# Attention and two MLPs on one core: the first decays' row transfers move from SyncE's queue to ScalarE's, and the loads of weights are released from waiting for them

## The chip, the cores and the metric

The kernel runs on one core of one Trainium2 chip. The metric is the device time of one execution in microseconds (us); lower is better.

## What is computed

For 4 batches of 8 heads, 576 positions and head size 64: scores = q k^T / 8 plus a decay, `cum[s] - cum[t]`, where `cum` is the running sum of `log(clip(f, 1e-4, 1))`; a causal mask; softmax; times v. The result is laid out as 2304 tokens of 512 values and goes through two MLPs:

```
scores = where(causal, -1e9, scale * q @ k.T + cum[:, None] - cum[None, :])
x = softmax(scores) @ v                                  # 2304 x 512
x = relu(x @ w_in).pow2 @ w_out                          # MLP 1, 512 -> 2048 -> 512
out = relu(x @ w2_in).pow2 @ w2_out                      # MLP 2
```

The weights arrive in 64 bit and are decoded to 32 bit by VectorE in the kernel.

## The kernel before, in words

**Matmuls.** Each number of an MLP is split into a high and a low part (fp32r), and three products of parts replace one. MLP 1 runs over groups of 256 tokens (`mlp_a`); for each of 16 tiles of 128 hidden units it does 12 matmuls (L844), a relu, square and split on ScalarE, GpSimd and VectorE, and 12 matmuls (L919). MLP 2 (L1213, L1239) follows in three units of 768 tokens.

**Stages of the attention.** The positions of a sequence are cut at 0, 64, 192, ... The first 64 positions of all heads are done by two calls of `first_part(y)` (y = 0, 1, two batches each), the next 128 by 16 calls of `pair`, the rest by 32 calls of `unit`. The two first parts together make the 256 tokens of MLP 1's group 0. The decay enters the scores as two more rows of q and k (rows 64 and 65 of a 66-row contraction): `load_qk` loads 64 rows (512 KB for each y), and `load_aug(r)` copies row 64 + r from `a0`, which lies on 32 partitions, to one partition (8 KB each, four in all). `a0` comes from `f` by clip, log (ScalarE), running sum (`scan0`, VectorE) and two multiplications by 8 and -8 (`times8`, L1325). After the scores (L481) a first part takes eight steps of softmax (L487 to L497), a transpose (L509) and its copy (L512), the product with v (L521), and the split into `xk` (L536 on ScalarE, L538 on VectorE). Then L844 can start on group 0.

**Weights.** `weights(i)`, i = 0 to 15, loads 1 MB (128 x 2048 words) with SyncE (L784), decodes it in three VectorE operations (L802, L804, L806), rounds on ScalarE (L819) and subtracts on VectorE (L823). Three staging tiles serve the loads. Loads 1 and 2 have `first_loads[:2]` as dependencies, the two transfers of y = 0's decay rows. Load 0 depends on `o_t`, the loading of ScalarE's first table. The `qk` loads of `pair` depend on all four decay transfers, and so does `store2`, which writes the pairs' decays to DRAM.

**The order of work.** Every operation is entered by `op(engine, duration, fn, priority, deps, buffers)`. `Plan.run` simulates the engines with these durations, and emits the instructions of each engine in the order in which they started in the simulation. The lowest priority number goes first: `U` is -1.0e9, the first parts stand at -1.0e8, load i of the weights at -459.5 + 133.3 i, the pairs at 201.5 i. An engine holds a slot free for an operation of priority below -1.0e7 only if that is ready within 0.1 us of simulated time. On the chip each engine runs its instructions in that fixed order. While the plan finds TensorE idle it puts in small matmuls that nobody reads (L1360).

Of the kernel before, what the change touches and what calls it, by code (L numbers as in the profile page):

```python
# [69 lines left out]
class Plan:  # L70
# [17 lines left out]
    def op(self, eng, dur, fn, prio, deps=(), uses=(), data=None, other=None, dmas=1, rows=128):  # L88


        o = Op()
        o.how, o.uses, o.data, o.dmas, o.rows, o.turn = {eng: (dur, fn, 0)}, tuple(uses), data, dmas, rows, dur == self.TURN[0]
        if other:
            o.how[other[0]] = (other[1], other[2], 1)
        o.prio = (prio, len(self.ops))
        o.outs, o.ready, o.nwait = [], 0.0, 0
        for d in deps:
            if d is not None:
                d.outs.append(o)
                o.nwait += 1  # L100
        for b in o.uses:
            b.left += 1
        self.ops.append(o)
        return o

    def run(self):
# [15 lines left out]
        while todo:  # L122
            again = True
            while again:
                again = False
                for e in engs:
# [60 lines left out]
                    end = t + dur + self.LAT[e]  # L187
                    if o.data is not None:

                        free[e] = t  # L190
                        _, a, z = self.TURN if o.turn else self.COPY
                        for _ in range(o.dmas):
                            at = max(free[e], lanes[issued % 8])
                            free[e] = at + dur / o.dmas
                            dge = max(dge, at) + a
                            dma = max(dma, dge + z) + o.data / o.dmas
                            end = lanes[issued % 8] = dma + self.LAT["DMA"] + (self.TURNED if o.turn else 0.0)
                            issued += 1
# [60 lines left out]
def attention_then_two_squared_relu_mlps(  # L259
# [15 lines left out]
    nc = tc.nc  # L275
# [177 lines left out]
    def first_part(y, prio):  # L453
# [10 lines left out]
            nc.sync.dma_start(out=room[y][0:64], in_=qk0[y])  # L464

        def load_aug(r):
            nc.sync.dma_start(out=qk_[64 + r:65 + r].rearrange("p n z s -> p n (z s)"),
                              in_=a0[2 * y * H:2 * y * H + 2 * H, r].rearrange("p z s -> p (z s)"))

        def load_v():  # L470
            nc.sync.dma_start(out=vv, in_=v0[y])

        l1 = op("SP", P.COPY[0], load_qk, U + y, first_loads[:2] if TUNE["q1"] else [], data=1.46)
        l2 = [op("SP", P.COPY[0], lambda r=r: load_aug(r), U + 1 + y, [aug_first], data=0.1) for r in range(2)]
        first_loads.extend(l2)
        l3 = op("SP", P.COPY[0], load_v, U + 3 + y, l2, data=0.73)

        def sc():
            for b, i, h in heads:
# [1 line left out]
                nc.tensor.matmul(bk()[64 * h:64 * h + 64, c:c + Q0], lhsT=qk_[:66, n, 0], rhs=qk_[:66, n, 1],  # L481
                                 start=True, stop=True, skip_group_check=True)

        e = op("PE", 1.24, sc, prio, [l1] + l2, [bk], rows=66)
        full = [128, H, Q0]
        steps = [
            ("DVE", dve(512), lambda: nc.vector.scalar_tensor_tensor(  # L487
# [34 lines left out]
                                 rhs=pT[rows, 128 * i + 64 * h:128 * i + 64 * h + 64],  # L522
                                 start=True, stop=True, skip_group_check=True)

        e = op("PE", 1.24, av, prio, [e, l3], [o, t], rows=64)
        first_done.append(e)

        for b in range(2):
# [17 lines left out]
    def pair(b, i, prio):  # L546


        h0 = 2 * i
        x, vv, pp, pT, bk, o = Buf(QKA), Buf(VV), Buf(PP), Buf(PTA), Buf(BK), Buf(BO)  # L550
        n = QA - Q0
        p0 = pos(b, Q0)

        def v_():
            return vv().rearrange("p n z d -> p (n z d)")[:, 0:3 * D].rearrange("p (n d) -> p n d", n=3)

        def load_qk():
            nc.sync.dma_start(out=x()[0:64], in_=qk[b, h0:h0 + 2, :, :QA].rearrange("h (z d) s -> d (h z) s", z=2))

        def load_aug():  # L560
            nc.sync.dma_start(out=x()[64:66], in_=aug2_d[:, b * H + h0:b * H + h0 + 2].rearrange("r h z s -> r (h z) s"))

        def load_v():
            nc.sync.dma_start(out=v_(), in_=v1[b, i])

        ld = op("SP", P.COPY[0], load_qk, prio, first_loads, [x], data=0.6)
        o_aug = op("SP", P.COPY[0], load_aug, prio, aug_second + [ld], [x], data=0.1)
        ov = op("SP", P.COPY[0], load_v, prio + TUNE["vd"], [ld], [vv], data=0.55)

        def sc():  # L570
            y = x()
            for h, c, k0, k1 in ((0, 0, 0, QA), (1, QA, 128, QA), (1, QA + 64, 0, 128)):
                nc.tensor.matmul(bk()[:, c:c + k1 - k0], lhsT=y[:66, 2 * h, Q0:QA], rhs=y[:66, 2 * h + 1, k0:k1],
                                 start=True, stop=True, skip_group_check=True)

        o_s = op("PE", 0.84, sc, prio, [ld, o_aug], [x, bk], rows=66)
        os_ = []
        for t in range(2):
            c = slice(QA * t, QA * t + QA)
            e = op("DVE", dve(QA) + 0.01, lambda t=t, c=c: max_of(pp, t, bk()[:, c], mask1[:, c], c.start),  # L580
                   prio, [o_s, o_m1], [bk, pp])
            os_.append(op("ACT", act(QA) + 0.18, lambda t=t: exp_of(pp, t, 128, QA * t, QA), prio, [e], [pp]))
        o_r = op("DVE", 0.07, lambda: recip(0, pp, 0, 2, 1.0), prio, os_, [pp])
        o_r = op("DVE", 0.08, lambda: recip(1, pp, 0, 2), prio, [o_r], [pp])

        def norm(eng, t):
            y, r = pp()[0][:, QA * t:QA * t + QA], pp()[3][:, t:t + 1]
            if eng == "ACT":
                nc.scalar.activation(out=y, in_=y, func=AF.Copy, scale=r)
            else:  # L590
                (nc.vector if eng == "DVE" else nc.gpsimd).tensor_scalar(out=y, in0=y, scalar1=r, scalar2=None, op0=ALU.mult)

        p_ops = [either(TUNE["pha"], *((e, d, lambda t=t, e=e: norm(e, t)) for e, d in (("ACT", act(QA) + 0.09), ("DVE", dve2(QA) + 0.06))),
                        prio, [o_r], [pp], c=("POOL", pool_(QA), lambda t=t: norm("POOL", t))) for t in range(2)]

        def tr():
            for j in range(3):
                c = slice(128 * j, 128 * j + 128)
                nc.tensor.transpose(o()[:, c], pp()[0][:, c], ident)

        def copy(eng):
            (nc.scalar.copy if eng == "ACT" else nc.vector.tensor_copy)(out=pT()[:, 0:384], in_=o()[:, 0:384])

        o_tr = op("PE", 0.375, tr, prio, p_ops, [pp, o])
        a_tr.append(o_tr)
        o_tr = either(TUNE["ev"], ("ACT", act(384, True), lambda: copy("ACT")), ("DVE", dve(384), lambda: copy("DVE")),
                      prio + TUNE["pz"], [o_tr], [o, pT])

        def av():
            y = pT()  # L610
            for h in range(2):
                rows, dst = slice(64 * h, 64 * h + 64), o()[64 * h:64 * h + 64, 384:512]
                nc.tensor.matmul(dst, lhsT=v_()[:, h], rhs=y[:, 256 * h:256 * h + 128],
                                 start=True, stop=False, skip_group_check=True)
                nc.tensor.matmul(dst[:, 64:128], lhsT=v_()[rows, 2], rhs=y[rows, 192:256],
                                 start=False, stop=True, skip_group_check=True)

        o_av = op("PE", 0.8, av, prio + TUNE["pq"], [o_tr, ov], [pT, vv, o])
        a_av.append(o_av)

        def fold(eng):
            dst = X[:, i, p0:p0 + n]
            (nc.scalar.copy if eng == "ACT" else nc.vector.tensor_copy)(out=dst, in_=o()[:, 384:512])

        e = either(TUNE["fa"], ("ACT", act(n, True), lambda: fold("ACT")), ("DVE", dve(n), lambda: fold("DVE")),
                   prio + TUNE["fo"], [o_av], [o])
        for g in groups(p0, p0 + n):
            fold_ops.setdefault((g, i), []).append(e)
# [144 lines left out]
    def weights(i, prio, prio2, deps, free, stage, words):  # L773
# [47 lines left out]
        def lo(eng):  # L821
# [1 line left out]
            eng.tensor_tensor(out=x[:, 1::2], in0=word(), in1=f32(x[:, 0::2]), op=ALU.subtract)  # L823

        o = either(2 if i < TUNE["ws"] else TUNE["wq"], ("SP", P.COPY[0], lambda: load(nc.sync)), ("ACT", 0.15, lambda: load(nc.scalar)),
                   prio, deps + (first_loads[:2] if i else []), [st], data=2.92 if wide else 1.46)
        if wide:
            for y in range(3 if t is not st else 4):
                o = op("DVE", dve2(1024) if y in ((0,) if t is not st else (0, 2)) else dvs(1024),
# [433 lines left out]
    with tc.manual_schedule():  # L1263
# [56 lines left out]
            nc.vector.tensor_tensor_scan(out=f_cum[:, 0:z], data0=f_log[:, 0:z], data1=zero.to_broadcast([nh_, z]), initial=0.0,  # L1320
                                         op0=ALU.add, op1=ALU.add)

        def times8(x, n):
            for i, m in enumerate((8.0, -8.0)):
                nc.vector.tensor_scalar(out=x[:, i, i], in0=f_cum[:, 0:n], scalar1=m, scalar2=None, op0=ALU.mult)  # L1325

        def scan0():
            scan(Q0)
            times8(a0, Q0)

        def scan1():
            scan(S)
# [35 lines left out]
        o = op("ACT", act(Q0), lambda: f_ln(0, Q0), U, [o])  # L1368
        o_f = op("DVE", dve2(S - Q0), lambda: f_clip(Q0, S), -1.0e7, [o_f])
        o_f = op("ACT", act(S - Q0), lambda: f_ln(Q0, S), U, [o_f])  # L1370
        op("ACT", 1.5, lambda: nc.scalar.activation(out=stat[:, 0, 0, 6:7], in_=stat[:, 0, 0, 7:8], func=AF.Exp), U, [o_f])
        aug_first = o = op("DVE", 0.45, scan0, U, [o, o_c])
        first_done, first_loads = [], []
        for y in range(2):
            first_part(y, -1.0e8 + y)
        o = op("DVE", 0.67, scan1, -1.0e7, [o_f])
        o_8 = op("ACT", 2 * act(QA), times8_act, -1.0e7, [o, o_m1])
        aug_second = [op("SP", P.COPY[0], store2, -1.0e7, [o_8] + first_loads, data=0.3)]
        o_p = op("ACT", act(S), lambda: parts(0), TUNE["PP"], [o] + first_done)
        o_p = op("DVE", dvs(S), lambda: parts(1), TUNE["PP"], [o_p])  # L1380
        o_p = op("ACT", 2 * act(S), lambda: parts(2), TUNE["PP"], [o_p])
# [116 lines left out]
```

## Time and profile before

| | us |
|---|---|
| runs | 997.28, 1000.00, 1002.94 (median 1000.0) |
| profiled execution | 1000.74 |
| its span, first to last instruction | 999.0 |
| TensorE busy | 969.2 |
| VectorE busy | 674.8 |
| ScalarE busy | 458.2 |
| GpSimd busy | 328.5 |
| mean granted clock | 0.986 of full |

A busy time is the sum over instructions, overlaps counted once; matmuls are pipelined, so that a busy TensorE is not one at its peak. The clock is the share of full speed that TensorE was granted.

### The profile page before, as it was taken

The numbers are of one execution on the slowest core, as the hardware profiler recorded it, in microseconds if no ns is written. First come the engines' busy times: TensorE is split into PE (matmuls) and PEld (weight loads), VectorE is DVE, ScalarE is ACT, GpSimd is POOL, SyncE is SP. The second block draws the span as 40 slices with busy tenths as digits, with TensorE's granted clock in tenths as the row PEclk, the third lists the DMA queues.
The fourth block names the chain that finished last, engine by engine and source line by source line (L and its number), as shares of the span: only waits on it lengthen the run. The fifth ranks groups of instructions, "written<-read, shape, count | busy, mean of one in ns | idle before, by whom it ended". The sixth has DMA issues, their size and how long they took to land.

```text
span 999.0 us, 17472 instructions
## 1 busy us (share of the span) xinstructions
PE 969.2 (97%) x6697; PEld 865.5 (87%) x6699; DVE 674.8 (68%) x1355; ACT 458.2 (46%) x894; POOL 328.5 (33%) x270
## 2 busy tenths in 40 slices
PE   5999999999999999999999999999999999999997
PEld 3788898788888888887999999898988989889896
DVE  6989666767667766666278689978684435844343
ACT  2776566778677767776333354222231112311111
POOL 2211242544243424334232343124252223522220
PEclk6999999999999999999999999999999999999999
DMA  9766146666656656655547712753333222232223
GB/s 266 241 190 234 43 96 127 131 123 132 142 109 140 148 108 140 127 118 119 115 148 231 234 43 89 271 195 120 127 114 140 70 78 64 87 104 68 77 67 106
DMA packets 172948, 131.93 MB, mean 132 GB/s; under 512 B 134784, under 2 KB 151424, under 8 KB 170688
## 3 DMA queue, kind: packets, MB, share of 16 engines
q1 hardware_dynamic: 172864, 130.81, 48.5%
q8 instruction: 53, 0.87, 0.4%
q14 instruction: 31, 0.25, 0.1%
HBM read 85.07 MB, written 18.42 MB: 104 GB/s over the span
## 4 chain that ended last, share of the span: by engine, by line
PE 38%; issue 7%; DVE 3%; POOL 3%; ACT 1%; DMA 0%; POOLq 0%; SPq 0%; DVEq 0%; ACTq 0%
PE hp L1213 13%; PE bk L1239 10%; PE yp L919 5%; PE hp L844 5%; PE yp L1239 5%; POOL g L1226 2%; DVE w L1102 1%; PE bk L740 1%; POOL gt L869 0%; DVE sq L856 0%; DVE X L1082 0%; ACT w L1100 0%; DVE w L1147 0%; DMA out_dram<-st 0%; DMA qk<-aug_d 0%
## 5 line engine op out<-in xcount | busy, mean ns | idle before, releaser
L919 PE MATMUL yp<-gt,w 128*128 128x256 f32 x1728 | 229.0, 281 | 1.4 <-POOL gt L869 1.4
L844 PE MATMUL hp<-xk,w 128*128 128x256 f32 x1728 | 224.4, 280 | 0.2 <-DVE w L823 0.2
L919 PEld LDWEIGHTS yp<-gt,w 128*128 128x128 f32 x1728 | 215.9, 188 | 2.9 <-POOL gt L869 1.8
L844 PEld LDWEIGHTS hp<-xk,w 128*128 128x128 f32 x1728 | 212.2, 188 | 1.0 <-DVE w L823 0.4
L869 POOL TENSOR_TENSOR gt<-sq,gt 128x512 fp32r<-128x512 f32 x72 | 100.3, 1393 | 208.7 <-ACT gt L866 193.3
L1239 PE MATMUL bk<-w,g 128*128 128x512 f32 x576 | 148.2, 394 | 0.2 <-POOL g L1226 0.2
L1226 POOL TENSOR_TENSOR g<-r,g 128x768 fp32r<-128x768 f32 x34 | 63.5, 1868 | 211.3 <-ACT g L1225 209.4
L1213 PE MATMUL hp<-w 128*128 128x384 f32 x630 | 125.1, 338 | 3.4 <-DVE r L1190 3.4
L1225 ACT CAST g<-r 128x768 fp32r<-128x768 f32 x48 | 40.1, 836 | 187.1 <-DVE r L1224 187.0
L1213 PEld LDWEIGHTS hp<-w 128*128 128x128 f32 x630 | 113.3, 190 | 11.1 <-issue 2.3
L1239 PEld LDWEIGHTS bk<-w,g 128*128 128x128 f32 x576 | 106.7, 188 | 17.8 <-POOL g L1226 0.6
L412 ACT ACTIVATE pp<-pp,stat 128x448 f32<-128x448 f32 (+1 forms) x128 | 78.4, 613 | 36.0 <-DVE stat L404 26.4
L434 DVE SCALAR_TENSOR_TENSOR ph<-pp,stat,ph 128x320 f16<-128x320 f32 (+2 forms) x96 | 71.0, 741 | 27.3 <-ACT ph L427 26.1
L404 DVE CUSTOM_DVE_ANT_0 pp<-bk,mask 128x448 f32<-128x448 f32 (+1 forms) x128 | 59.9, 472 | 40.4 <-PE bk L700 38.7
L1190 DVE TENSOR_TENSOR r<-hp,st 128x384 f32<-128x384 f32 x64 | 35.5, 555 | 67.9 <-PE hp L1213 67.8
L1224 DVE SCALAR_TENSOR_TENSOR r<-r 128x768 f32<-128x768 f32 x48 | 78.4, 1632 | 1.5
L740 PE MATMUL bk<-pt,vv 64*128 64x64 f16 (+7 forms) x672 | 78.1, 254 | 0.0
L1213 PE MATMUL hp<-w,far 128*128 128x384 f32 x378 | 74.4, 335 | 0.0
L1239 PE MATMUL yp<-w,g 128*128 128x512 f32 x288 | 74.4, 393 | 0.0
L427 ACT ACTIVATE ph<-pp,stat 128x320 f16<-128x320 f32 (+2 forms) x96 | 63.8, 665 | 17.8 <-DVE stat L421 13.7
L1213 PEld LDWEIGHTS hp<-w,far 128*128 128x128 f32 x378 | 67.3, 188 | 4.9
L740 PEld LDWEIGHTS <-vv 128*128 128x128 bf16 (+3 forms) x672 | 37.1, 101 | 39.6 <-issue 25.6
(170 smaller groups left out, 1227.3 us busy)
## 6 DMA issues: line engine op xcount, KB each, us to landing
w<-wo_d SPq DMA_DIRECT2D x48, 512.0 KB
stage<-in_w_dram SPq DMA_DIRECT2D x26, 512.0 KB
raw<-in_qk_dram SPq DMA_DIRECT2D x32, 288.0 KB
wo_d<-part SPq DMA_DIRECT2D x16, 512.0 KB
st<-in_w_dram SPq DMA_DIRECT2D x7, 1024.0 KB
ph<-in_w_dram SPq DMA_DIRECT2D x7, 1024.0 KB
vv<-in_v_dram SPq DMA_DIRECT2D x32, 160.0 KB
qk_a<-in_qk_dram SPq DMA_DIRECT2D x16, 192.0 KB
```

The source lines that it names most:

```text
L404: nc.vector.tensor_tensor_reduce(out=x[:rows, c0:c0 + wd], in0=src, in1=msk, scale=-0.125, scalar=3.0e38 if first else nmax[:rows, 5:6], o ...
L412: nc.scalar.activation(out=x, in_=x, func=AF.Exp, scale=-1.0, bias=nmax[:rows, t:t + 1], accum_out=ssum[:rows, t:t + 1])
L427: nc.scalar.activation(out=a, in_=x, func=AF.Copy, scale=r)
L434: nc.vector.scalar_tensor_tensor(out=flat[:rows, z:z + wd], in0=x, scalar=r, in1=flat[:rows, 128 * blk:128 * blk + wd], op0=ALU.mult, op1= ...
L740: nc.tensor.matmul(dst.rearrange("p (n c) -> p n c", n=rh.shape[1]), lhsT=lt, rhs=rh, start=(i == 0), stop=(i == len(todo) - 1), skip_grou ...
L844: nc.tensor.matmul(ps, lhsT=lt, rhs=rh, start=(k_ == 0 and c == 0), stop=(k_ == KD - 1 and c == 2))
L869: eng.tensor_tensor(out=gt[1]()[:, :c], in0=sq()[:, :c], in1=f32(gt[0]()[:, :c]), op=ALU.subtract)
L919: nc.tensor.matmul(yp[d // 2]()[:, d % 2], lhsT=lt, rhs=rh, start=(i == 0 and c == 0 and d % 2 == 0), stop=(i == NF - 1 and c == 2), skip_ ...
L1213: nc.tensor.matmul(ps()[:, 0:TH], lhsT=lt, rhs=rh, start=(k_ == 0 and c == 0), stop=(k_ == 1 and c == 2))
L1224: o = op("DVE", dvs(TU), lambda r=r: nc.vector.scalar_tensor_tensor(out=r(), in0=r(), scalar=0.0, in1=r(), op0=ALU.max, op1=ALU.mult), e0, ...
L1226: l = either_vp(TU, lambda e, r=r, g=g: e.tensor_tensor(out=g()[:, 1], in0=r(), in1=f32(g()[:, 0]), op=ALU.subtract), e0, [h], [r, g])
L1239: nc.tensor.matmul(bank(ob[c]), lhsT=g()[:, a, c * 128:(c + 1) * 128], rhs=rw()[:, b], start=(p == 0 and x == 0 and z == 0), stop=(p == NP ...
```

## The change

The four decay transfers are issued by ScalarE. Row 64's needs VectorE's multiplication, row 65's needs a new one on ScalarE (`scan0_act`). No load of weights, no `qk` load of a pair and no `store2` depends on them any more; `v0[y]` follows the plan's landing of `qk0[y]`. Load 0 of the weights has priority U + 0.5 in place of -459.5. The load of ScalarE's Exp table goes to U + 1.5. Four durations in the plan are lowered: the scores and the product with v of a first part, and the transposes and the product with v of a pair. In the planner a transfer that isn't issued by SyncE occupies its engine for the duration given and does not pass through the simulated transfer queue.

```diff
-                    if o.data is not None:
+                        if e != "SP":
+                            end = t + dur + o.data + self.LAT["DMA"]
+                    if o.data is not None and e == "SP":
 ...
-            nc.sync.dma_start(out=qk_[64 + r:65 + r].rearrange("p n z s -> p n (z s)"),
+            nc.scalar.dma_start(out=qk_[64 + r:65 + r].rearrange("p n z s -> p n (z s)"),
 ...
-        l1 = op("SP", P.COPY[0], load_qk, U + y, first_loads[:2] if TUNE["q1"] else [], data=1.46)
-        l2 = [op("SP", P.COPY[0], lambda r=r: load_aug(r), U + 1 + y, [aug_first], data=0.1) for r in range(2)]
-        first_loads.extend(l2)
-        l3 = op("SP", P.COPY[0], load_v, U + 3 + y, l2, data=0.73)
+        l1 = op("SP", P.COPY[0], load_qk, U + y, data=1.46)
+        l2 = [op("ACT", P.COPY[0], lambda r=r: load_aug(r), U + y, [aug_first[r]], data=0.1) for r in range(2)]
+        l3 = op("SP", P.COPY[0], load_v, U + 3 + y, [l1], data=0.73)
 ...
-        e = op("PE", 1.24, sc, prio, [l1] + l2, [bk], rows=66)
+        e = op("PE", 0.92, sc, prio, [l1] + l2, [bk], rows=66)
 ...
-        e = op("PE", 1.24, av, prio, [e, l3], [o, t], rows=64)
+        e = op("PE", 0.55, av, prio, [e, l3], [o, t], rows=64)
 ...
-        ld = op("SP", P.COPY[0], load_qk, prio, first_loads, [x], data=0.6)
+        ld = op("SP", P.COPY[0], load_qk, prio, [], [x], data=0.6)
 ...
-        o_tr = op("PE", 0.375, tr, prio, p_ops, [pp, o])
+        o_tr = op("PE", 0.26, tr, prio, p_ops, [pp, o])
 ...
-        o_av = op("PE", 0.8, av, prio + TUNE["pq"], [o_tr, ov], [pT, vv, o])
+        o_av = op("PE", 0.53, av, prio + TUNE["pq"], [o_tr, ov], [pT, vv, o])
 ...
-                   prio, deps + (first_loads[:2] if i else []), [st], data=2.92 if wide else 1.46)
+                   prio if i else U + 0.5, deps, [st], data=2.92 if wide else 1.46)
 ...
-        def times8(x, n):
-            for i, m in enumerate((8.0, -8.0)):
-                nc.vector.tensor_scalar(out=x[:, i, i], in0=f_cum[:, 0:n], scalar1=m, scalar2=None, op0=ALU.mult)
-
         def scan0():
             scan(Q0)
-            times8(a0, Q0)
+            nc.vector.tensor_scalar(out=a0[:, 0, 0], in0=f_cum[:, 0:Q0], scalar1=8.0, scalar2=None, op0=ALU.mult)
+
+        def scan0_act():
+            nc.scalar.mul(out=a0[:, 1, 1], in_=f_cum[:, 0:Q0], mul=-8.0)
 ...
-        op("ACT", 1.5, lambda: nc.scalar.activation(out=stat[:, 0, 0, 6:7], in_=stat[:, 0, 0, 7:8], func=AF.Exp), U, [o_f])
-        aug_first = o = op("DVE", 0.45, scan0, U, [o, o_c])
-        first_done, first_loads = [], []
+        op("ACT", 1.5, lambda: nc.scalar.activation(out=stat[:, 0, 0, 6:7], in_=stat[:, 0, 0, 7:8], func=AF.Exp), U + 1.5, [o_f])
+        o = op("DVE", 0.45, scan0, U, [o, o_c])
+        aug_first = [o, op("ACT", 0.2, scan0_act, U, [o])]
+        first_done = []
 ...
-        aug_second = [op("SP", P.COPY[0], store2, -1.0e7, [o_8] + first_loads, data=0.3)]
+        aug_second = [op("SP", P.COPY[0], store2, -1.0e7, [o_8], data=0.3)]
```

## Rows read from the trace of the kernel before

**Rows 1.** The page, part 1: busy time, share of the span, instructions.
```profile
PE 969.2 (97%) x6697; PEld 865.5 (87%) x6699; DVE 674.8 (68%) x1355; ACT 458.2 (46%) x894; POOL 328.5 (33%) x270
```

**Rows 2.** Busy time by stretch: length, each engine's busy us, clock, DMA share, GB/s.
```profile
0.00:31.40 31.40, 19.71 (x174) 11.36 (x177) 22.78 (x38) 10.51 (x23) 6.94 (x21) 0.67 0.84 250
31.40:103.50 72.10, 71.36 (x541) 62.82 (x539) 67.01 (x146) 52.18 (x134) 11.15 (x7) 1.00 0.69 221
103.50:999.00 895.50, 878.15 (x5983) 791.35 (x5983) 585.00 (x1174) 395.47 (x740) 310.40 (x242) 1.00 0.46 121
```

**Rows 3.** Waits of TensorE over the span: releaser, us in total, times, longest.
```profile
PE bk L481 <- DMA tmp<-tmp: 7.3, 1, 7.3
PE bk L700 <- DMA qk<-aug_d: 5.0, 4, 1.8
...
PE hp L844 <- DVE w L823: 0.2, 1, 0.2
```

**Rows 4.** SyncE's queue in order of time: start, us, line, transfer.
```profile
0.74 0.41 SPq L1275 DMA_DIRECT2D tmp<-in_f_dram  x1
1.21 1.20 SPq L464 DMA_DIRECT2D tmp<-in_qk_dram  x2
2.45 0.58 SPq L784 DMA_DIRECT2D st<-in_w_dram  x1
5.47 2.51 SPq L467 DMA_DIRECT2D tmp<-tmp  x4
8.02 1.05 SPq L471 DMA_DIRECT2D tmp<-in_v_dram  x2
...
12.63 0.35 SPq L784 DMA_DIRECT2D ph<-in_w_dram  x1
13.03 0.43 SPq L784 DMA_DIRECT2D tmp<-in_w_dram  x1
```

**Rows 5.** VectorE in order of time, its first 34 us.
```profile
2.67 1.05 DVE L1311 TENSOR_SCALAR tmp<-tmp 32x64 f32<-32x64 f32 x2 [1.50 <-DMA tmp<-in_f_dram]
...
4.23 1.25 DVE L1325 TENSOR_SCALAR tmp<-tmp 32x64 f32<-32x64 f32 x2
...
12.64 0.69 DVE L802 TENSOR_SCALAR tmp<-st 128x1024 uint32<-128x1024 uint32 x1 [5.41 <-DMA st<-in_w_dram]
...
15.77 0.68 DVE L487 SCALAR_TENSOR_TENSOR tmp<-bk,mask 128x512 f32<-128x512 f32 x1
...
18.83 0.68 DVE L487 SCALAR_TENSOR_TENSOR tmp<-bk,mask 128x512 f32<-128x512 f32 x1
...
31.53 0.48 DVE L538 TENSOR_TENSOR xk<-hp,xk 128x128 fp32r<-128x128 f32 x2
```

**Rows 6.** ScalarE in order of time, its first 34 us.
```profile
4.40 1.28 ACT L1371 ACT_TABLE_LOAD   x1
...
15.89 1.04 ACT L819 CAST w<-tmp 128x1024 fp32r<-128x1024 f32 x1 [8.01 <-DVE tmp L806]
```

**Rows 7.** TensorE in order of time, 12 to 33 us.
```profile
13.14 3.68 PE L481 MATMUL bk<-tmp 66*64 66x64 f32 x64 [7.33 <-DMA tmp<-tmp]
...
31.46 1.73 PE L844 MATMUL hp<-xk,w 128*128 128x256 f32 x10
```

**Rows 8.** Busy time by stretch, as rows 2, of 2.5 us each.
```profile
7.50:10.00 2.50, 0.00 (x0) 0.00 (x0) 0.00 (x0) 0.38 (x2) 0.00 (x0) 0.59 0.94 311
10.00:12.50 2.50, 0.00 (x0) 0.00 (x0) 0.00 (x0) 0.00 (x0) 0.00 (x0) 0.50 1.01 241
```

**Rows 9.** Waits of VectorE between 31 and 104 us, the longest.
```profile
DVE X L623 <- PE bk L615: 2.6, 2, 1.7
```

**Rows 10.** TensorE in order of time around one pair's product with v.
```profile
65.13 0.43 PE L613 MATMUL bk<-pt,vv 128*64 128x128 f32 x2
...
66.37 0.55 PE L599 MATMUL bk<-ident,pp 128*128 128x128 f32 x3
66.67 1.66 PE L919 MATMUL yp<-gt,w 128*128 128x256 f32 x12
```

More of the change, by code (lines that the diff above doesn't have):

```diff
@@ L466, in load_aug @@
         def load_aug(r):
-            nc.sync.dma_start(out=qk_[64 + r:65 + r].rearrange("p n z s -> p n (z s)"),
-                              in_=a0[2 * y * H:2 * y * H + 2 * H, r].rearrange("p z s -> p (z s)"))
+            nc.scalar.dma_start(out=qk_[64 + r:65 + r].rearrange("p n z s -> p n (z s)"),
+                                in_=a0[2 * y * H:2 * y * H + 2 * H, r].rearrange("p z s -> p (z s)"))
         def load_v():
             nc.sync.dma_start(out=vv, in_=v0[y])
-        l1 = op("SP", P.COPY[0], load_qk, U + y, first_loads[:2] if TUNE["q1"] else [], data=1.46)
-        l2 = [op("SP", P.COPY[0], lambda r=r: load_aug(r), U + 1 + y, [aug_first], data=0.1) for r in range(2)]
-        first_loads.extend(l2)
-        l3 = op("SP", P.COPY[0], load_v, U + 3 + y, l2, data=0.73)
+        l1 = op("SP", P.COPY[0], load_qk, U + y, data=1.46)
+        l2 = [op("ACT", P.COPY[0], lambda r=r: load_aug(r), U + y, [aug_first[r]], data=0.1) for r in range(2)]
+        l3 = op("SP", P.COPY[0], load_v, U + 3 + y, [l1], data=0.73)
         def sc():
```

## The prediction

> **What bounds the kernel now.** I read the busy times first: TensorE is busy for 969.2 of 999.0 us [rows 1], so only stretches in which it lacks work, or in which its work comes late, can move the time. The table by stretch shows three stages [rows 2]. Up to 31.4 us TensorE has little to do (19.71 us, fillers included), at a mean clock of 0.67. From 31.4 to 103.5 us it is busy for 71.36 of 72.10 us, and VectorE for 67.01: MLP 1's group 0 and the pairs run here, and each of the 16 weight tiles must first pass VectorE. After 103.5 us TensorE is busy for 878.15 of 895.50 us, while no other engine is near its limit. So the change, which lies in the first 31 us, is worth what it moves the start of L844, as far as VectorE delivers the weights for it.
>
> What sets that start? The list of TensorE's waits has one long entry: the first scores, L481, wait 7.3 us for the decay rows [rows 3]. SyncE's queue shows why: the four small transfers are issued from 5.47 to 7.98 us behind 0.07 MB of f, 1 MB of qk0 and 1 MB of weights on the same queue [rows 4], and the scores start at 13.14 [rows 7]. Meanwhile the transfer engines are 0.94 to 1.01 busy at 311 and 241 GB/s and no compute engine but ScalarE does anything [rows 8]. VectorE sits idle 5.41 us until tile 0 of the weights has landed at 12.64; from there it has no gap to speak of, and it is VectorE's last operation of the first part y = 1, at 31.53, that releases L844 [rows 5, 7].
>
> **The change, part by part.**
>
> *Issue of the small transfers.* They need VectorE's multiplication, whose two instructions stand from 4.23 to 5.48 [rows 5]. One goes to ScalarE, but the other remains, and I take its end as 5.4: the issue starts no earlier than now. ScalarE is free for it, since the Exp table (1.28 us at 4.40 [rows 6]) goes behind. Four issues at 2.51 / 4 = 0.63 us [rows 4] end at 6.7 for y = 0 and 7.9 for y = 1. Those 2.5 us, the table load after them (to 9.2) and the new multiplication are hidden: ScalarE is idle for 8.01 us up to 15.89 [rows 6]. Without that cover the Exp of the first softmax would be later by up to 1.28 + 2.51 us.
>
> *Landing.* No transfer of ScalarE's queue stands in the trace. Lower bound: f's transfer ends its issue at 1.15 and is read at 2.67, so 1.5 us, into idle engines. Upper bound: what they take now, 13.14 - 7.98 = 5.2 us [rows 4, 5, 7]. I take 2.0, near the first, because they leave the queue that the large ones stand in. So y = 0's rows are there at 8.7 and y = 1's at 9.9.
>
> The Trainium skill ("DMA: Bandwidth & Descriptors", Queues, rings and completion order) says that SyncE and ScalarE each have one ring on each of the same 16 DMA engines, and that an engine takes turns between rings by packets; by that the landing is near the lower bound. The same page (Issuing engines are not separate DMA queues) says that issuing from several engines saves only the issue time; by that the small transfers still share saturated engines, the landing is at the upper bound and the gain goes. This trace has one queue only, so it shows neither.
>
> *Scores and softmax.* The clock is at 0.50 from 10 us on [rows 8], so each y takes 3.68 / 2 = 1.84 us [rows 7]: y = 0 from 8.7 to 10.5, y = 1 to 12.4. VectorE's first step for y = 1 is then at about 12.6 instead of 18.83. From that step to the end of L538 it now takes 31.53 + 0.48 - 18.83 = 13.2 us [rows 5], which would put L844 at 25.8. But SyncE's order changes: by the planner's numbers SyncE has issued f and both qk0 loads at 3 x 0.55 = 1.65 us, when load 0 of the weights still waits for the table (0.4 + 0.16 + 1.5 + 0.18 = 2.24), so load 1, now free, goes ahead of load 0. Then load 2, three pairs' qk and only then v0. Load 1 lands where load 0 did, at about 12.6, and load 0 1 MB later, 3 to 4 us at 311 to 266 GB/s (266 is the page's mean for the first slice). Its decode, at priority U + 0.5, is placed among the softmax steps instead of before them; it takes 15.77 - 12.64 = 3.1 us. Bounds: 25.8 if it takes the place of the decodes that stand there now, 28.9 if all of it is added. I take 27.4: L844 starts 4.1 us earlier (2.6 to 5.7).
>
> *v0.* It moves behind f, qk0, three tiles and three pair loads (192 KB each): 4.9 MB with itself, at 266 GB/s about 18.5 us plus a start of 1. The product with v of y = 0 comes at about 23, so it is hidden; a landing later than that would cost its lateness one for one.
>
> *Weights against TensorE up to 103.5.* VectorE starts at 10.7 with the first softmax, not at 12.64, so it gains 1.9 us of its idle time. At the end of this stage TensorE waits 0.2 us for the last weight split [rows 3]: both engines arrive together, so a gain of 4.1 on one and 1.9 on the other is worth 1.9 to 4.1. VectorE has 5.1 us of slack in that stage, 2.6 of it waiting for TensorE's pair products [rows 2, 9], which come earlier too; I take 3.0.
>
> *The other waits removed* (pairs' qk, `store2`) free work that is needed only after 28 us; I cost them at nothing.
>
> *The new durations in the plan* change the order of everything behind. One pair's product with v takes 66.37 - 65.13 = 1.24 us and its transposes 66.67 - 66.37 = 0.30 [rows 10]; the plan now says 0.53 and 0.26 instead of 0.80 and 0.375. So the plan runs further ahead of TensorE, by (0.27 + 0.115) x 16 = 6.2 us more. That costs nothing as long as TensorE is the one behind. What a new order can give or cost is bounded by the present waits on late transfers, 5.0 us in four units [rows 3]: gone, or twice as long. I take 0 and keep 2.5 each way.
>
> **Sum.** 999.0 + 1.74 around the span = 1000.74; minus 3.0 is 997.7. The profiled run is 0.74 above the median of the runs, so 997.0 as a median.
>
> **Rivals.**
> *A, the full gain.* The decode of tile 0 is hidden, L844 starts at 25.8 or before, and VectorE's slack is used up: 5.7 us, and 1 or 2 more from a luckier order: 993. For it: VectorE idles 5.41 us now. Against it: the last split at 103.5.
> *B, given back.* L844 starts early, but the weights come as late as before, because three staging tiles and VectorE's 93% pace them, and TensorE waits later by what it gained: 1000. For it: rows 2 and 3, and the plan running ahead. Against it: VectorE's share of the 5.41 us is real work done earlier.
> *C, slower: the freed weights crowd the small transfers.* Place: the 16 transfer engines from 5 to 18 us. Before, 2.1 MB stood ahead of the decay rows; now f, qk0, three tiles and three pair loads, 4.65 MB, are issued by about 6 us. If the small ones complete only as that backlog does, they land at about 18 us at 266 GB/s, and L844 comes 18 - 13.1 = 4.9 us later than now: 1005. It is slower as soon as the rows land after 13.1. For it: engines 0.94 to 1.01 busy, and a transfer ends with its slowest engine. Against it: separate queue, 32 KB in all. The skill's sentence on issuing engines above would lead to this case or to B.
>
> **Chances.** About 0.5%, 5 us, is what a measurement here can tell from no change. Forecast 0.45, with 994 to 1000 as its own range; A 0.20 (990 to 995); B 0.20 (999 to 1002); C 0.15 (1002 to 1007). Faster by over 0.5%: A nearly whole and the lower edge of the forecast, 0.19 + 0.09 = 0.28. Slower by over 0.5%: the upper two thirds of C and a bad order elsewhere, 0.13. The rest 0.59. The range that leaves out a tenth on either side is 990.5 to 1004.5.
>
> **What would show it.** Right: L467's four issues on ScalarE from about 5.4; L481 at 8.7 and not 13.14; L487 on VectorE at about 10.7 and idle time before it near 3.5 instead of 5.41; the second load issued of SyncE's L784 at about 2.9 instead of 12.63; the first L844 at 27 to 28; the last split of weights near 100.5. Wrong landing: L481 at 13 or later. Wrong on VectorE: a wait of L802 for a weight tile in the middle of the softmax, more than 2 us long. Given back: L844 early, but new waits of L844 for L823 before 103 us. The forecast fails as a whole if the time moves without L844's start moving, for then the order of the later stages did it.

## The result: 1.2% slower, and the profile after

The changed kernel takes 1012.65 us (four runs, 1011.15 to 1013.37) against 1000.8 us of the kernel before on the same chip: a ratio of 1.0119, interval 1.009 to 1.0148. I forecast 997.0 and a range up to 1004.5. TensorE's busy time grew by 7 us only, against 12.2 us of span [rows 1]:

```profile
PE 976.0 (97%) x6695; PEld 871.6 (86%) x6695; DVE 669.5 (66%) x1343; ACT 462.0 (46%) x905; POOL 321.9 (32%) x271
```

ScalarE in order of time: the four transfers are issued when I said, from 5.47 us, and the Exp table follows them.

```profile
5.47 2.50 ACTq L471 DMA_DIRECT2D tmp<-tmp  x4
8.00 1.28 ACT L1374 ACT_TABLE_LOAD   x1 [3.48 <-DVE tmp L1324]
```

TensorE in order of time (L485 is L481 of before, L848 is L844). The first scores start at 12.72, not at 8.7; group 0's first matmuls at 33.80, 2.3 us later than in the profiled run of before [rows 7], not 4.1 us earlier. Both starts vary between executions: in e7 and e8 below, whose orders are those of before up to 47 us, the scores start at 12.65 and 12.61 and L844 at 30.02 and 29.95, where the profiled run of before has 13.14 and 31.46.

```profile
12.72 3.68 PE L485 MATMUL bk<-tmp 66*64 66x64 f32 x64 [7.06 <-DMA tmp<-tmp]
...
33.80 1.76 PE L848 MATMUL hp<-xk,w 128*128 128x256 f32 x12
```

SyncE's queue: loads 1 and 0 of the weights now go out at 2.45 and 3.08, load 2 at 6.26 [rows 4].

```profile
2.45 0.58 SPq L788 DMA_DIRECT2D st<-in_w_dram  x1
3.08 0.43 SPq L788 DMA_DIRECT2D ph<-in_w_dram  x1
6.26 0.33 SPq L788 DMA_DIRECT2D tmp<-in_w_dram  x1
11.76 1.98 SPq L562 DMA_DIRECT2D qk_a<-in_qk_dram  x3
13.78 1.08 SPq L475 DMA_DIRECT2D tmp<-in_v_dram  x2
```

VectorE in order of time. Its order comes from a plan in which the scores arrive at 7 to 9 us. So after one step of a decode it waits at the softmax's first step for 2.66 us, with the rest of the decode queued behind; with the 4.24 us ahead it idles 6.9 us, where before it idled 5.41 [rows 5].

```profile
11.46 0.69 DVE L806 TENSOR_SCALAR tmp<-st 128x1024 uint32<-128x1024 uint32 x1 [4.24 <-DMA st<-in_w_dram]
14.81 0.69 DVE L491 SCALAR_TENSOR_TENSOR tmp<-bk,mask 128x512 f32<-128x512 f32 x1 [2.66 <-PE bk L485]
15.42 1.22 DVE L808 SCALAR_TENSOR_TENSOR tmp<-st,tmp 128x1024 uint32<-128x1024 uint32 x1
```

**Where the 12 us are.** In windows of 10 us over the span I added what TensorE loses: time without work, and busy time multiplied by the missing part of its granted clock. Before: 29.8 + 10.0 = 39.8 us; after: 35.0 + 17.7 = 52.7. The difference, 12.9, is the span's 12.2 within the error of such a sum. By stretch it lies between 30 and 150 us, the stage of the pairs and the weights. There the table by stretch has, first before, then after:

```profile
30.00:150.00 120.00, 118.01 (x933) 105.69 (x934) 97.01 (x219) 80.87 (x195) 31.05 (x31) 1.00 0.53 161
```
```profile
30.00:150.00 120.00, 112.30 (x814) 97.99 (x815) 82.44 (x177) 71.69 (x180) 22.62 (x26) 0.93 0.50 157
```

Before, 2.0 us are lost; after, 7.7 us without work and 112.3 x 0.07 = 7.9 us of clock, and 119 matmuls fewer are done by 150 us. The largest piece lies between 85 and 102.5 us. TensorE from 84 us on, after:

```profile
83.83 0.52 PE L848 MATMUL hp<-xk,w 128*128 128x256 f32 x3
84.18 0.93 PE L577 MATMUL bk<-qk_a 66*128 66x192 f32 x6
84.95 0.49 PE L603 MATMUL bk<-ident,pp 128*128 128x128 f32 x3
86.01 0.43 PE L617 MATMUL bk<-pt,vv 128*64 128x128 f32 x2 [0.57 <-ACT pt L606]
...
88.12 0.49 PE L603 MATMUL bk<-ident,pp 128*128 128x128 f32 x3
89.82 0.43 PE L617 MATMUL bk<-pt,vv 128*64 128x128 f32 x2 [1.20 <-DVE pt L606]
...
93.20 2.91 PE L923 MATMUL yp<-gt,w 128*128 128x256 f32 x12
...
98.08 2.93 PE L923 MATMUL yp<-gt,w 128*128 128x256 f32 x12
```

and before, in the same stretch:

```profile
84.78 0.49 PE L599 MATMUL bk<-ident,pp 128*128 128x128 f32 x3
85.03 1.66 PE L919 MATMUL yp<-gt,w 128*128 128x256 f32 x12
86.61 0.43 PE L613 MATMUL bk<-pt,vv 128*64 128x128 f32 x2
...
87.85 1.69 PE L919 MATMUL yp<-gt,w 128*128 128x256 f32 x12
89.38 1.58 PE L844 MATMUL hp<-xk,w 128*128 128x256 f32 x12
...
91.81 1.66 PE L844 MATMUL hp<-xk,w 128*128 128x256 f32 x12
```

Before, a block of 12 MLP matmuls stands between a pair's transposes (L599) and its product with v (L613), and covers the copy that the product waits for. After, the steps of three pairs stand together from 84.2 to 93.2 us with no MLP matmul among them, and TensorE waits 0.57 and 1.20 us for copies. By stretch (length, busy us, clock), the granted clock then goes to the lower level:

```profile
85.00:87.50 2.50, 1.93 (x14) 1.00 0.92 383
87.50:90.00 2.50, 1.30 (x11) 1.00 0.45 117
90.00:92.50 2.50, 2.50 (x14) 0.71 1.04 344
92.50:95.00 2.50, 2.50 (x13) 0.50 0.52 195
95.00:97.50 2.50, 2.50 (x12) 0.50 0.00 0
97.50:100.00 2.50, 2.50 (x13) 0.50 0.50 92
100.00:102.50 2.50, 2.50 (x17) 0.74 0.82 334
```

There the same 12 matmuls of L923 take 2.9 instead of 1.7 us. These two waits and the lower clock up to 102.5 us take 6.9 us, half of what is lost between 30 and 150; the rest lies in smaller pieces. Group 0 ends (its copy out of PSUM on ScalarE, before and after) 14.8 us later; behind 150 us TensorE loses as much as before, 19.6 against 19.4 us:

```profile
123.31 0.58 ACT L933 COPY st<-yp 128x512 f32<-128x512 f32 x1 [1.56 <-PE yp L919]
```
```profile
138.15 0.58 ACT L937 COPY st<-yp 128x512 f32<-128x512 f32 x1
```

### The profile page after: what moved, and what is told of

Its sections match the earlier page's. It is cut to its first block, busy times and chain, and to the rows that moved or that the text cites. A ratio compares the mean times of both kernels' runs of the same rounds, so it can differ in the third digit from the quotient of the medians.

```text
span 1011.2 us, 17464 instructions
## 1 busy us (share of the span) xinstructions
PE 976.0 (97%) x6695; PEld 871.6 (86%) x6695; DVE 669.5 (66%) x1343; ACT 462.0 (46%) x905; POOL 321.9 (32%) x271
## 4 chain that ended last, share of the span: by engine, by line
PE 72%; issue 9%; DVE 8%; DMA 4%; POOL 3%; ACT 2%; SPq 0%; POOLq 0%; ACTq 0%; DVEq 0%
PE yp L923 15%; PE hp L848 15%; PE hp L1217 12%; PE bk L1243 10%; PE bk L744 7%; PE bk L704 5%; PE yp L1243 5%; POOL g L1230 2%; DMA stage<-in_w_dram 2%; PE bk L577 1%; DVE w L1106 1%; PE bk L617 1%; POOL gt L873 1%; DVE w L1151 1%; DVE sq L860 1%
## 5 line engine op out<-in xcount | busy, mean ns | idle before, releaser
L923 PE MATMUL yp<-gt,w 128*128 128x256 f32 x1728 | 232.5, 283 | 4.3 <-POOL gt L873 4.3
L848 PE MATMUL hp<-xk,w 128*128 128x256 f32 x1728 | 225.5, 281 | 2.6 <-DVE w L827 1.3
L923 PEld LDWEIGHTS yp<-gt,w 128*128 128x128 f32 x1728 | 218.8, 191 | 7.1 <-POOL gt L873 6.0
L848 PEld LDWEIGHTS hp<-xk,w 128*128 128x128 f32 x1728 | 213.0, 189 | 4.1 <-DVE w L827 1.5
L873 POOL TENSOR_TENSOR gt<-sq,gt 128x512 fp32r<-128x512 f32 x72 | 96.0, 1334 | 203.3 <-ACT gt L870 203.2
L1243 PEld LDWEIGHTS bk<-w,g 128*128 128x128 f32 x576 | 106.7, 188 | 17.7 <-POOL g L1230 0.6
L408 DVE CUSTOM_DVE_ANT_0 pp<-bk,mask 128x448 f32<-128x448 f32 (+1 forms) x128 | 60.1, 473 | 52.7 <-PE bk L704 41.3
L857 ACT ACTIVATE sq<-hp 128x512 f32<-128x512 f32 x72 | 42.9, 595 | 60.6 <-PE hp L848 57.0
```

The lines of the kernel that those rows point to most:

```text
L408: nc.vector.tensor_tensor_reduce(out=x[:rows, c0:c0 + wd], in0=src, in1=msk, scale=-0.125, scalar=3.0e38 if first else nmax[:rows, 5:6], o ...
L848: nc.tensor.matmul(ps, lhsT=lt, rhs=rh, start=(k_ == 0 and c == 0), stop=(k_ == KD - 1 and c == 2))
L873: eng.tensor_tensor(out=gt[1]()[:, :c], in0=sq()[:, :c], in1=f32(gt[0]()[:, :c]), op=ALU.subtract)
L923: nc.tensor.matmul(yp[d // 2]()[:, d % 2], lhsT=lt, rhs=rh, start=(i == 0 and c == 0 and d % 2 == 0), stop=(i == NF - 1 and c == 2), skip_ ...
L1243: nc.tensor.matmul(bank(ob[c]), lhsT=g()[:, a, c * 128:(c + 1) * 128], rhs=rw()[:, b], start=(p == 0 and x == 0 and z == 0), stop=(p == NP ...
```

## The experiments

Three theories on where the loss comes from. Theory 1: the lowered durations in the plan put the order out of step. Theory 2: the plan believes in a landing at 7 us that is 12.7 on the chip. Theory 3: any new order costs something, because the one before is a good one. Beside them stands my rival C, that the freed weights crowd the small transfers. Each measured ratio is to the kernel before on the same chip, with its 95% interval.

**e1, the durations alone**, on the kernel before (lines shortened):

```diff
-        e = op("PE", 1.24, sc      -> +  0.92
-        e = op("PE", 1.24, av      -> +  0.55
-        o_tr = op("PE", 0.375, tr  -> +  0.26
-        o_av = op("PE", 0.8, av    -> +  0.53
```

> The kernel before with nothing of the change but the four lowered durations in the plan. Theory 1 (the lowered durations of a pair, 0.53 and 0.26 where the trace of before has 1.24 and 0.30, put the order of the pairs' stage out of step): most of the loss is here, 1007 to 1013, with stretches at half clock between 80 and 120 us and the last split of weights near 120 us instead of 103.6. Theory 2 (the plan believes that the small transfers land at about 7 us, and they land at 12.7): no loss from here, 998 to 1003. Theory 3 (any new order costs some us, whichever edit makes it): 1001 to 1010, with no tie to a place.

1008.88 us, ratio 1.0075 (1.0051 to 1.0099). The time is as theory 1 says, the place is not: L844 starts 3 us earlier, at 28.44, and the loss is spread over 30 to 90 and 150 to 360 us, with no half clock between 80 and 120.

**e2, the changed kernel with the old durations** (the four lines above, backwards).

> The changed kernel with the four durations of before. Theory 1: the loss goes, 998 to 1003. Theory 2: the loss stays, 1008 to 1014, L844 starts at 33 to 34 us again. Theory 3: 1001 to 1010.

1010.08, ratio 1.01 (1.0062 to 1.0138). So what remains of the change loses by itself too, as theory 2 has it; L848 starts at 35.18. The two parts don't add: +8.7 and +9.9 make 18.6, and both together cost 11.9.

**e3, the waits restored** in the changed kernel (lines shortened; `first_loads` is filled again as before):

```diff
-                   prio if i else U + 0.5, deps, [st]
+                   prio if i else U + 0.5, deps + (first_loads[:2] if i else []), [st]
-        ld = op("SP", P.COPY[0], load_qk, prio, [], [x]
+        ld = op("SP", P.COPY[0], load_qk, prio, first_loads, [x]
```

> The changed kernel, but loads 1 and 2 of the weights wait again for the first two small transfers and the pairs' qk loads for all four; the small transfers stay on ScalarE's queue. If the 2 MB of freed weights crowd the small transfers, the first scores start well before 12.7 us here, at 8 to 10. If the 2.1 MB that were issued ahead of them in both kernels (f, qk0, tile 0) are enough, they start at 12 to 13 again. Theory 1: 1007 to 1013, as the durations stay. Theory 2: with early scores 1000 to 1005; with scores at 12.7 it stays above 1005.

1009.64, ratio 1.008 (1.0052 to 1.0108), scores at 12.88 and, for y = 1, at 17.58. Holding the loads back brings nothing: the freed weights were not what delays the scores. SyncE issued v0 early here, at 3.10, so 2.6 MB were ahead.

**e4, the plan told of the landing**:

```diff
-        l2 = [op("ACT", P.COPY[0], lambda r=r: load_aug(r), U + y, [aug_first[r]], data=0.1) for r in range(2)]
+        l2 = [op("ACT", P.COPY[0], lambda r=r: load_aug(r), U + y, [aug_first[r]], data=5.2) for r in range(2)]
```

> The changed kernel with one number of the plan corrected: a small transfer on ScalarE takes 5.1 us longer there, so that the plan's scores start at about 12.3 us, near the 12.7 of the trace; the transfers themselves and their issue are unchanged. Theory 2: the wait of 2.7 us on VectorE for the scores goes, L844 starts at 31 us or before and the time falls to 1000 to 1005. Theory 1: the stage after 33 us stays slow, 1007 to 1013. Theory 3: anything from 1000 to 1012.

1006.38, ratio 1.005 (1.003 to 1.007). Over half of the loss goes, and with it VectorE's wait for the scores, but L848 starts later still, at 35.59. So it goes not by the start, as theory 2 had it, and the time lies between what theories 1 and 2 gave.

The next four separate the chip's part from the plan's.

**e5, the queue alone.** Only `nc.sync` becomes `nc.scalar` in `load_aug`; the operation stays SyncE's in the plan, so every other order is that of before. With the small transfers off its queue, SyncE issues v0 at 3.10 instead of 8.02, so 2.6 MB are ahead of them.

> The kernel before with its plan and every engine's order kept, except that the four small transfers go out on ScalarE's queue, at the place that the plan of before gives them there. So no order changes but the queue. If the separate queue helps the small transfers, the first scores start before 13.1 us and the time falls by up to 3 us, 996 to 1000; if the shared transfer engines hold them, the scores start at 12 to 14 us and the time stays 999 to 1002. Theory 3 (a new order of the later work costs the time, not the queue): no loss, below 1003.

1000.35, ratio 0.9999 (0.9983 to 1.0015), scores at 12.69. With the old queue they start at 12.65 and 12.61 in e7 and e8, so the other queue alone moves neither the scores nor the time.

**e6, queue and release**: e5's line and the following, with the orders of PE, VectorE, ScalarE and GpSimd kept (shortened, without an assertion):

```diff
+            if i in (1, 2):
+                return
             eng.dma_start(out=dst, in_=src)
+            if i == 0:
+                for j, x in zip((1, 2), sorted(WHOLE.free, key=lambda x: x[1])):
+                    eng.dma_start(out=x[2][:, 0:2048].bitcast(U32), in_=w[0, j].rearrange("p z c -> p (z c)").bitcast(U32))
```

> As the queue alone, and SyncE issues loads 1 and 2 of the weights right behind load 0 at about 3 us instead of waiting for the small transfers; PE, VectorE, ScalarE and GpSimd keep the order of before. That is what the change says it does, without a new plan. If the freed weights crowd the small transfers, the first scores come later than 13.1 us (up to 18) and the time rises by up to 5 us, 1001 to 1006. If not, the scores stay at 12 to 14 us and the time at 998 to 1002. Theory 3: below 1004, well under the 1012 of the changed kernel.

1001.59, ratio 1.0011 (0.9995 to 1.0028), scores at 12.76, with 4.1 MB issued ahead of the small transfers instead of 2.1. With the old order, what the change does to these transfers costs and gains nothing, and rival C falls. The release of the pairs' loads and of `store2` is not in e6; e9 has it. The 12 us come with the new order.

**e7 and e8, neutral orders**: the kernel before with a pair's product at 0.78 instead of 0.80, and with its transposes at 0.385 instead of 0.375.

> The kernel before with one number of the plan moved by 0.02: a pair's product with v is 0.78 instead of 0.80. No transfer, queue or wait is touched, only the order that comes out of the plan behind about 45 us. Theory 3 (the order of before is an unusually good one, and any other costs some us): 1003 to 1011. Theories 1 and 2: 998 to 1003.

1001.35, ratio 1.0004 (0.9981 to 1.0028).

> The kernel before with one number of the plan moved the other way: a pair's transposes are 0.385 instead of 0.375. Theory 3: 1002 to 1011 again, though at another place in the stage than the other neutral order. Theories 1 and 2: 998 to 1003.

996.83, ratio 0.9974 (0.9958 to 0.999): faster than both kernels. Both change the order from 47 us on, VectorE's and ScalarE's most, so theory 3 falls in the form that any new order costs some us. Two orders don't show how much another one may cost.

**e9, landing and old durations** (e4's line, and e2's four).

> The changed kernel with both corrections to the plan at once: small transfers that land at about 12.3 us, and the four durations of before. If the two errors of the plan are the whole loss (each alone left 1006 to 1010), 998 to 1003, and TensorE's idle time and time at half clock between 30 and 150 us fall to the 2 us of before from 15.9. If any plan with the new start of the kernel loses, whatever it believes, 1005 to 1010 again.

1001.13, ratio 1.0008 (0.9986 to 1.0029). In time the loss is gone, with the change's queue, release and start. Its place is not as I expected: by the same sum TensorE still loses 7.2 us between 30 and 150, not 2. (e6 loses 7.8 there, at a time that can't be told from before either.)

**e10, landing, and the trace's durations for a pair** (`tr` 0.30, `av` 1.24; the first parts' stay at 0.92 and 0.55).

> The changed kernel with the landing corrected and the pair's durations set to the trace's: 1.24 for the product with v and 0.30 for the transposes. If a truthful plan is what is missing, this is the best of the changed kernels, 994 to 1002. If the loss comes from what any new order does, 1002 to 1010.

1001.53, ratio 1.0008 (0.9978 to 1.0038). Against e4 only the pair's two numbers differ, and the ratio falls by 0.42%, with intervals that overlap. Summed by windows of 10 us, TensorE loses 0.7 us between 30 and 150 here, after the changed kernel's 15.9. It is not better than before, and "best of the changed kernels" holds only as a tie with e9, whose durations are the old ones.

**e11, the pair's two durations alone**, on the kernel before.

> The kernel before with only the pair's two durations lowered (0.53 and 0.26), those of the first parts kept. The first 30 us then keep the order of before. If the pair's durations carry the loss of the durations (8.7 us with all four): 1006 to 1011. If the first parts' durations carry it: 998 to 1003.

1001.66, ratio 1.0018 (1.0002 to 1.0034): the pair's numbers alone carry little of e1's loss.

**e15, the first parts' two durations alone.**

> The kernel before with only the two durations of the first parts lowered (0.92 and 0.55). The pair's two alone left 1001.7 and all four 1008.9. If the first parts' durations carry the loss, 1006 to 1010, with idle time and half clock between 30 and 180 us. If only the four together do, 998 to 1003, and the loss belongs to that one order and to no number.

1006.09, ratio 1.0054 (1.0032 to 1.0077). So of e1's 0.75% some 0.54% come with the first parts' numbers and 0.18% with the pair's (e11); within the intervals that is all of it. The scores' lowered number is the one that fits the trace: 1.84 us at half clock is 0.92 at full [rows 7], and `Plan.run` itself doubles a duration where it takes the clock to be at half. The longer numbers may have made up for the landing that the plan has too early; no run tests that.

**e12, all loads of weights behind the small transfers, in the plan.**

> The changed kernel, but every load of weights, tile 0 too, waits in the plan until the four small transfers have landed, so that only f and qk0 (1.1 MB) and v0 (0.5 MB) are issued ahead of or beside them. If transfers already issued on the other queue are what holds the small ones, the first scores start at 8 to 10 us instead of 12.7; if ScalarE's queue itself is slow, at 12 to 13. The time is 1000 to 1012: tile 0 comes later, and the order is new again.

1007.85, ratio 1.0053 (1.0021 to 1.0086). It doesn't test what it was for: the wait exists only in the plan, on the chip SyncE issued v0 at 2.47 and tile 0 at 3.57, ahead of the small transfers; scores at 13.65.

**e13, tile 0 really behind them**: its `dma_start` is kept back and issued by the last `load_aug`; the transfers are on SyncE's queue, as before, and all other orders are those of before.

> The kernel before with its plan and every other engine's order kept; on SyncE's queue the load of tile 0 of the weights goes behind the four small transfers instead of ahead of them, so that only f and qk0 (1.1 MB) are under way when these are issued at 5.47. In every run so far, with 2.1 to 4.1 MB issued ahead on the other queue, no packet of ScalarE's queue moved before 10 us. If bytes issued earlier are what holds the small transfers, the first scores start at 9 to 10 us here. If something else does (a fixed time of some 5 us until the first packet), they start at 12 to 13 again. VectorE's order has tile 0's decode ahead of the softmax, and tile 0 lands at 13 to 15, so the time is 999 to 1004 either way.

1001.82, ratio 1.0016 (0.9989 to 1.0043). SyncE's queue and the scores:

```profile
5.47 2.51 SPq L468 DMA_DIRECT2D tmp<-tmp  x4
8.03 0.58 SPq L789 DMA_DIRECT2D st<-in_w_dram  x1
```
```profile
9.29 3.68 PE L485 MATMUL bk<-tmp 66*64 66x64 f32 x64 [3.12 <-DMA tmp<-tmp]
```

With 1.1 MB ahead instead of 2.1 the scores start at 9.29, from the old queue. So on SyncE's queue it is bytes issued earlier that hold the small transfers. For ScalarE's queue no run shows it, since none has less than 2.6 MB ahead. The time doesn't follow: VectorE's order still has tile 0's decode first, this starts at 13.22, and L844 at 32.11.

**e14**, the same on e8's order.

> The same on top of the order that the transposes' 0.385 gave (996.8 us, the fastest so far): 995 to 1000, by the start of L844 against 29.95 us there.

997.58, ratio 0.9964 (0.9946 to 0.9982), L844 at 31.25 against 29.95 in e8: as fast as e8, no more.

**e16 and e17, an early start that the plan knows**: load 0 depends on `aug_first` beside `o_t`; e17 has the four durations at 0.92, 0.55, 0.30 and 1.24 besides.

> The kernel before, with load 0 of the weights depending in the plan on the same running sum as the small transfers, so that SyncE issues it behind them and the plan knows it. The scores start at 9 to 10 us as in e13, and VectorE's order can now put the softmax ahead of tile 0's decode, which e13 could not. If an early start is worth what the prediction gave it, L844 starts at 27 to 29 and the time is 994 to 998; if the new order of the later stages takes it back, as it did in e1 (L844 at 28.4 and 1008.9), 999 to 1009.

1006.71, ratio 1.0051 (1.002 to 1.0082), scores at 9.37, L844 at 27.86. The early start is there and the gain is not.

> The same with the four durations set near the trace's (0.92, 0.55, 0.30 and 1.24). If a plan that is right on the landing and on the durations is what gets the early start through, 992 to 998; if what an order is worth can't be told from how right its numbers are, anything from 996 to 1009.

1002.31, ratio 1.0013 (0.9986 to 1.0039). TensorE and then ScalarE:

```profile
27.38 1.66 PE L844 MATMUL hp<-xk,w 128*128 128x256 f32 x12
```
```profile
122.48 0.59 ACT L933 COPY st<-yp 128x512 f32<-128x512 f32 x1 [1.55 <-PE yp L919]
```

L844 starts at 27.38, where I had forecast it, 4.1 us ahead of the profiled run of before and 2.6 ahead of e7 and e8; group 0 ends 0.8 us ahead of before. The time misses the 992 to 998 of a plan that is right on landing and durations. TensorE's longest waits from 27 to 125 us, where the kernel before waits 0.7 us at most:

```profile
PE hp L844 <- DVE w L823: 2.0, 1, 2.0
PE bk L573 <- DVE stat L404: 0.9, 1, 0.9
PE bk L599 <- ACT pp L589: 0.8, 1, 0.8
```

## Why the prediction was wrong, step by step

*Issue of the small transfers*: right, 5.47 to 7.97 us.

*Landing*: wrong. I took 2.0 us after the issue, "because they leave the queue that the large ones stand in". They took 4.8 (7.97 to 12.72), near the upper bound, and 4.7 to 4.8 in e5 and e6 as well. The queue was left, the 16 transfer engines not: they were busy with SyncE's bytes. By queue (q1 is SyncE's, q10 ScalarE's; packets, MB, share of the engines), from 9 to 10 and from 10 to 11 us:

```profile
q1 hardware_dynamic: 49, 0.40, 96.1%
```
```profile
q1 hardware_dynamic: 63, 0.39, 103.1%
q10 hardware_dynamic: 47, 0.02, 6.9%
```

No packet of q10 moves before 10 us, 4.5 us after the first issue. What its first packet waits for is open. In all nine runs with the small transfers on ScalarE's queue it comes between 10.3 and 10.6 us, when q1 has moved 2.1 to 2.2 MB, whether 2.6 MB (e5) or 4.1 MB (e6) had been issued ahead. So they do pass bytes that SyncE issued earlier: in e6, from 0 to 12.7 us, when its scores start, q1 has moved 3.0 of the 4.1 MB:

```profile
q1 hardware_dynamic: 449, 2.97, 81.4%
q10 hardware_dynamic: 119, 0.03, 1.3%
```

A fixed time of ScalarE's queue is not excluded; in e10 the issue starts 0.4 us earlier, at 5.07, and the first packet comes no earlier, which speaks against it. My lower bound was too high: on SyncE's queue, with 1.1 MB ahead, the landing took 1.3 us (e13, 7.98 to 9.29).

The two rules of the Trainium skill that I weighed ("DMA: Bandwidth & Descriptors") come out so: Issuing engines are not separate DMA queues agrees with this trace (scores at 12.72, and at 12.6 to 13.1 from the old queue); the taking of turns between rings (Queues, rings and completion order) shows from 10 us on only, when both queues move packets (63 and 47 from 10 to 11 us).

*Scores and softmax*: wrong as a consequence. With scores at 12.72, VectorE's first step for the softmax is at 14.81 instead of 10.7, and its idle time 6.9 us instead of 3.5. That load 1 would go ahead of load 0, and land first, was right. Two readings of mine were wrong. The priority U + 0.5 holds for load 0 alone; the decode of tile 0 stays at -459.5. And L844 starts at 31.46, ahead of L538's last step at 31.53, so that step doesn't release its start, and the stretch that I took as 13.2 us is 12.6.

*v0*: hidden, as said; nothing waits for it.

*Weights against TensorE*: misread. I took 103.5 us as the last weight split. That is the last of one form of the instruction; tile 15 is split in another buffer, at 110.05 us before and at 125.03 after.

*What an early L844 is worth*: wrong as far as it was tried. I took 3.0 of 4.1 us. e17 has the 4.1 us, and its time can't be told from before; e16 has 3.6 and is slower. Each also has a new order behind it, so the early start alone was not priced. In e17 TensorE then waits 2.0 us for a weight split (L823), as rival B had it, and I gave that 0.20.

*The new durations* and the new order: this step failed with the largest size. "I take 0 and keep 2.5 each way" stands against +8.7 us for the durations alone (e1) and +9.9 for the rest of the new plan (e2). I had bounded a new order by the waits on late transfers of the units [rows 3]. The loss is elsewhere, between 30 and 150 us, 15.9 us against 2.0: half of it in one place, where pairs stand together without MLP matmuls between them, TensorE waits for copies and the granted clock is at 0.50 behind that. "That costs nothing as long as TensorE is the one behind" missed that TensorE has to have work in its order that is ready. The sign that I had named for this, a time that moves without L844's start, came out: 2.3 us of start against 12.2 us of span. A bad order had only a share of the 0.13 for slower.

*Rival C* had the sign but not the cause: e6 shows no crowding.

**What is shown and what is open.** Shown: with the old order the queue and the release cost nothing (e5, e6), and in another new order the whole change costs nothing (e9). So the loss comes with this order. The landing corrected in the plan, with other durations for a pair than the change's, takes it away (e9, e10); the landing alone leaves 0.5% (e4), and the old durations alone leave 1.0% (e2).

Not shown: that the plan's errors are the reason. Each corrected number also gives a new order. e9, with the old durations, is as fast as e10, and e17, whose plan was to be right on both, gains nothing. That e9 and e10 happened to get good orders, and e1 to e4 bad ones, is not excluded.

Open: what in these orders loses the time. The longest stretch without MLP matmuls between 36 and 136 us is 8.9 us in the changed kernel and 3.6 before. In e1 to e4, which are slower, it is 3.7 to 5.2 us, and in e6 and e17, which are not, 5.0 and 5.8. So the bunching belongs to the changed kernel alone, and doesn't account for the others. No one number is the cause either: on the kernel before, the first parts' numbers cost 0.54% (e15); with the landing corrected they stay lowered and cost nothing (e10).

## What to carry to other kernels

Where a planner writes the order of in-order engines, a change to a transfer or to a duration is two changes: measure its physical part with the order held fixed (e5, e6), then the new order. Here another queue brought the small transfers nothing (e5), and issuing them ahead of the last 1 MB brought their reader forward by 3.3 to 3.9 us (e13). The two queues behind a longer backlog were not compared. And before pricing an earlier start, look for what the next stage waits for once it starts early.

## What the runs showed that I had not expected

- A 0.010 us change of one number in the plan made the kernel 0.26% faster (0.9974, 0.9958 to 0.999), some 3 us from the order alone; one of 0.02 us moved it by no more than the noise (1.0004).
- Two small waits in a stretch of pair matmuls, 0.57 and 1.20 us, were followed by some 10 us at half clock, with TensorE busy throughout from 90 us. Half of 10 us is more than the waits themselves.
- With 2.6 and 4.1 MB issued ahead of the small transfers on ScalarE's queue the scores start at the same time (12.69, 12.76). On SyncE's queue, from 2.1 to 1.1 MB, their start moved from 13.14 to 9.29 (12.6 in e7 and e8). What holds them is thus not simply all that stands in the other queue; how much of it does was not measured.
